# A gated linear attention and an ELU layer on one core: weights' range tested from a second reading, logarithm sums ahead of the arctangent, state products in another order

## The chip, the cores and the metric

The kernel runs on one core of a Trainium2 chip. The metric is the device time of one execution in microseconds (us). Two kernels are compared, the one before the change and the one after it. The engines are TensorE (PE; its weight loads are listed as PEld), VectorE (DVE), ScalarE (ACT), GpSimd (POOL) and the queue of SyncE (SP), which issues most DMAs. All five run their own instructions in order and wait for each other by semaphores.

## The reference

For 4 batches, 8 heads, 768 positions and 48 channels a complex gate with modulus at most 0.999 carries a 48 x 48 state, and the layer behind it is an ELU between two matrices whose entries are 64-bit floats:

```python
mag = np.sqrt(a_re * a_re + a_im * a_im)
scale = np.minimum(mag, 0.999) / (mag + 1e-06)
a_re_n, a_im_n = (a_re * scale, a_im * scale)
for t in range(S):
    new_re = ar * S_re - ai * S_im
    new_im = ar * S_im + ai * S_re
    S_re, S_im = (new_re + k_t v_t^T, new_im)
    y[:, :, t] = q_t^T S_re
x = y.transpose(0, 2, 1, 3).reshape(3072, 384)
h = x @ w_in                                  # 384 x 2048, float64
g = np.where(h > 0.0, h, np.exp(np.minimum(h, 0.0)) - 1.0)
out = (g @ w_out).astype(np.float32)          # 2048 x 384, float64
```

## The kernel before, in words

The work is cut into 12 units: a unit u is two batches (n = 0, 1) by 128 positions with all eight heads. The state runs through the units of the same batches in chunks of 64 positions. For each unit the kernel

- loads a (`load_a`), q and k (`load_qk`) and v (`load_v`), each as [128, 2 x 8 x 48] float32;
- turns the gate into a logarithm of its modulus and an angle: `squares` (two squares on ScalarE, their sum on VectorE or GpSimd), `logarithms` (two logarithms and two exponentials on ScalarE, then two products, L622 and L623, on VectorE for units 0 and 1 and on GpSimd for the others), `slopes` (L629 and L632 on VectorE), `noted` (two reductions on VectorE that keep the least real part and the largest imaginary part), `angles` (arctangent on ScalarE), `carried` (L660 on VectorE, adds the angle carried over from the unit before);
- sums angles along the positions (`turns`: matmuls L671 with a triangular matrix, then L676 and L679 on VectorE) and logarithms (`decays`: matmuls L693, four exponentials L698 on ScalarE), takes sine and cosine (`waves`), and multiplies q and k by them (`gated`: L724, L726, q on VectorE, k on GpSimd);
- then, for n = 0 and 1: `transposed` of q and k (PE L746, copied by ScalarE L747; called Tq and Tk in the prediction), `scores` (L754, masked by L759 on VectorE), `states` (L775; L786 on VectorE adds the old state, L787 on GpSimd multiplies it by the decay), `values` (L797 and L804, copied by ScalarE), and `seam` (six small DMAs from GpSimd's queue that put the output into the layout of the next matmul);
- the layer: eight `hidden` steps (L838: 12 matmul records into a PSUM tile `mlp` with three buffers; ELU by L843 and L844 on ScalarE and L845 on VectorE), and eight `project` steps (L854, 8 matmul records).

The matrices are read as pairs of 32-bit words. `fetch` loads one of 14 parts (six of w_in with 1024 columns, eight of w_out with 768 columns) into a staging tile, and `rounded` makes it float32: five instructions on VectorE (L570, L574, L579, L583, L586). With them goes a range test, so that entries below about 2**-15 in the high word's reading, taken as a float32, become zero: ScalarE squares the high words in place (L578), GpSimd compares (L587) and multiplies the result by it (L590). `rounded` is a generator, and `converts(n)` runs it for n steps; `fetches(n)` starts the next n loads.

The order of all instructions is written out by hand. `put(at, fn, ...)` notes a call at a slot, the calls are sorted by slot (ties in the order of noting), and each engine gets its instructions in that order. A unit from 2 on takes 16 slots, in each of which one `hidden` or `project` step of an earlier unit stands. Units 0 and 1 have negative slots, since nothing of the layer can run beside them; the first `hidden` step is in slot 4, the first `project` in slot 20, and Tq of unit 2 in slot 22. In the plan before, unit u's `squares`, `logarithms`, `slopes`, `noted`, `angles`, `carried`, `turns`, `waves`, `decays` and `gated` stand at r + 11, 12, 14, 14, 15, 15, 16, 17, 18 and 19 with r = 16 (u - 2), and its transposes and products from r + 22 on. A `verdict` at the end takes the noted least and largest values; if they are out of range, a general version of the whole kernel (`_general`) runs behind a branch. With these inputs it does not.

Staging tiles, the `g` tiles of the ELU output and the small tiles of the gate (`n`, six buffers) share tags and therefore buffers; `ar`, `ai`, `q` and `k` have one buffer each.

Of the kernel before, what the change touches and what calls it, by code (L numbers as in the profile page):

```python
# [20 lines left out]
LEAST_RE = 0.7  # L21
# [2 lines left out]

TOP, LOW = 0xC0000000, 0x07FFFFFF
F32_EXP = 0xFF800000

LEAST_SQ = 2.0**-30  # L30
WC = 1024
WF = 2


LEVELS = [1, 2, 4, 8, 16, 32, 64]
# [399 lines left out]


@with_exitstack
def kernel(
    ctx: ExitStack,
    tc: tile.TileContext,  # L440
# [47 lines left out]
    least = cst.tile([C, NU], FP32, name="least")  # L488
    most = cst.tile([C, NU], FP32, name="most")
    ln_eps = value(float(np.log(2 * EPS)), "ln_eps")  # L490
    quarter = value(float(np.pi / 2), "quarter")

    def work(shape):
        return ps.tile(shape, FP32, tag="w", bufs=3, name="w")
# [28 lines left out]
        load(u, "v", v, 2, pad=True)  # L523

    G = HP - D
    places = [(j, i, j * HP, (2 * i + j) * D, D) for i in range(NI) for j in range(2)]
    places += [(j, i, j * HP + D, (2 * NI + j) * D + i * G, G) for i in range(NI) for j in range(2)]  # L530
    raw = {}

    def weights_of(kind, m):

        if kind == "in":
            i, f = m % NI, m // NI * WC
            dst = w_in[:, i, f : f + WC]
            t = sb.tile([C, WC, 2], U32, tag="g" + str(m // 2 % 2), bufs=2, name="w64")
            words = t.rearrange("p n two -> p (n two)")
            pairs = [  # L540
                (words[ds(at, n)], moe_w_in[ds(row, n), 2 * f : 2 * (f + WC)])
                for j, i1, at, row, n in places if i1 == i
            ]
        else:
            dst = w_out[:, ts(m, WF)].rearrange("p f n -> p (f n)")
            tag = "w64" if m % 4 < 2 else "g1"
# [12 lines left out]

    def rounded(kind, m):  # L560

        w, dst = raw.pop((kind, m))
        n = dst.shape[-1]
        lo, hi = w[:, :, 0], w[:, :, 1]
        f = sb.tile([C, n], U32, tag="wt", bufs=2, name="wf")
        p = sb.tile([C, n], U32, tag="wt", bufs=2, name="wp")
        yield nc.vector.tensor_scalar(  # L570
            out=f, in0=hi, scalar1=LOW, scalar2=3, op0=ALU.bitwise_and,
            op1=ALU.logical_shift_left,
        )
        yield nc.vector.scalar_tensor_tensor(  # L574
            out=f, in0=hi, scalar=TOP, in1=f, op0=ALU.bitwise_and, op1=ALU.bitwise_or
        )
        size = hi.bitcast(FP32)
        nc.scalar.activation(out=size, in_=size, func=AF.Square)  # L578
        yield nc.vector.tensor_scalar(  # L579
            out=p, in0=f, scalar1=F32_EXP, scalar2=None, op0=ALU.bitwise_and  # L580
        )
        f, p = f.bitcast(FP32), p.bitcast(FP32)
        yield nc.vector.scalar_tensor_tensor(  # L583
            out=p, in0=lo, scalar=2.0**-52, in1=p, op0=ALU.mult, op1=ALU.mult
        )
        yield nc.vector.tensor_tensor(out=dst, in0=p, in1=f, op=ALU.add)  # L586
        yield nc.gpsimd.tensor_scalar(  # L587
            out=size, in0=size, scalar1=LEAST_SQ, scalar2=None, op0=ALU.is_ge
        )
        nc.gpsimd.tensor_tensor(out=dst, in0=dst, in1=size, op=ALU.mult)  # L590


    def flat(t):
# [2 lines left out]
    def products(u):  # L596

        return nc.vector if u < 2 else nc.gpsimd

    def new(tag, bufs=1, shape=None):  # L600
        return sb.tile(shape or [C, NB, H, D], FP32, tag=tag, bufs=bufs, name=tag)

    def squares(u):
        x = nat[u]
        ar, ai = x["ar"], x["ai"]
        x["m2"], sq = new("n", 6), new("n", 6)
        nc.scalar.activation(out=x["m2"], in_=ar, func=AF.Square)
        nc.scalar.activation(out=sq, in_=ai, func=AF.Square)  # L608
        products(u).tensor_tensor(out=x["m2"], in0=x["m2"], in1=sq, op=ALU.add)  # L609

    def logarithms(u):


        x = nat[u]
        ar, ai = x["ar"], x["ai"]
        lm, lr = x["m2"], new("n", 6)
        nc.scalar.activation(out=lm, in_=lm, func=AF.Ln)
        nc.scalar.activation(out=lr, in_=ar, func=AF.Ln)
        e, x0 = new("n", 6), new("n", 6)
        nc.scalar.activation(out=x0, in_=lr, func=AF.Exp, scale=-1.0)  # L620
        nc.scalar.activation(out=e, in_=lm, func=AF.Exp, scale=-0.5, bias=ln_eps)
        products(u).tensor_tensor(out=lr, in0=ar, in1=x0, op=ALU.mult)  # L622
        products(u).tensor_tensor(out=x0, in0=ai, in1=x0, op=ALU.mult)  # L623
        x["e"], x["w"], x["t"] = e, lr, x0

    def slopes(u):
        x = nat[u]
# [236 lines left out]

    def verdict():

        fit, ones = cst.tile([C, NU], FP32, name="fit"), value(1.0, "ones")
        nc.vector.tensor_scalar(
            out=fit, in0=least, scalar1=LEAST_RE, scalar2=None, op0=ALU.is_ge
        )  # L870
        nc.vector.scalar_tensor_tensor(
            out=fit, in0=most, scalar=LEAST_RE, in1=fit, op0=ALU.is_le, op1=ALU.mult
        )
        t = work([1, NU])
# [3 lines left out]
        nc.vector.tensor_scalar(  # L878
            out=needs, in0=n, scalar1=C * NU - 0.5, scalar2=None, op0=ALU.is_lt
        )  # L880


# [42 lines left out]
    def put(at, fn, *args):  # L925
        plan.append((at, len(plan), lambda: fn(*args)))

    def decays_of(u, *at):
        for x, fn in zip(at, (squares, logarithms, slopes, noted, angles, carried)):
            put(x, fn, u)  # L930

    def gates_of(u, *at):
        for x, fn in zip(at, (turns, waves, decays, gated)):
            put(x, fn, u)

    def values_of(u, base):
        for n, at in enumerate([[0, 1, 2, 3, 5], [3, 4, 6, 7, 8]]):
            for x, (fn, *args) in zip(at, (
                (transposed, u, "q", n), (transposed, u, "k", n), (scores, u, n),
                (states, u, n), (values, u, n),  # L940
            )):
                put(base + x, fn, *args)
        put(base + 9, seam, u)
# [30 lines left out]
    for at, n in FETCHES:  # L974
        put(at, fetches, n)
    for at, n in CONVERTS:
        put(at, converts, n)
# [4 lines left out]
    with tc.If(nc.values_load(needs[0:1, 0:1]) > 0):  # L982
        _general(tc, q, k, v, a_re, a_im, w_in, w_out, out)


# [30 lines left out]
```

## Time and profile before

| | |
|---|---|
| median of 3 runs | 831.32 us (829.62 to 831.35) |
| profiled execution | 831.39 us, its span 829.6 us |
| mean granted TensorE clock | 0.952 |
| busy: PE, DVE, ACT, POOL | 720.4, 336.2, 403.0, 307.4 us |
| read from HBM, written | 36.55 MB, 4.79 MB |

The span is from the first to the last instruction. A busy time is the time in which an engine executes; for PE it is partly modelled. A row of a group has its line, engine and operation, the tiles (output <- inputs), shapes and count; then busy time and mean ns of one, then idle time of the engine just before and what ended it. A row of the order in time has start and duration in us and, in brackets, the idle time before it and what released it.

### The profile page before, as it was taken

How to read it: one execution, taken by the hardware profiler on the slowest of the kernel's cores; microseconds unless marked ns; L12 is line 12 of the kernel's file. 1: busy time of each engine (PE TensorE's matmuls, PEld its weight loads, DVE VectorE, ACT ScalarE, POOL GpSimd, SP SyncE). 2: the span in 40 equal slices, each digit the busy share in tenths (PEclk: the TensorE clock that was granted, in tenths of full speed). 3: DMA queues.
4: the chain of work that ended last, by engine and by line, in shares of the span. 5: the costliest groups of instructions: out<-in, count | busy, mean ns of one | idle time of the engine just before them, and what ended most of it. 6: DMA issues, size and time to landing. Idle time of an engine off the chain costs nothing.

```text
span 829.6 us, 12975 instructions
## 1 busy us (share of the span) xinstructions
PE 720.4 (87%) x5406; PEld 532.3 (64%) x5406; DVE 336.2 (41%) x378; ACT 403.0 (49%) x604; POOL 307.4 (37%) x233
## 2 busy tenths in 40 slices
PE   1586438678999999999999999999999999999996
PEld 0465326555658758668668578577577587587773
DVE  4779998743143152242242342332432332331020
ACT  6663214752554554555555655555455556442130
POOL 0436796703343342441540540541541441340100
PEclk9866678889999999999999999999999999999999
DMA  9969425032042042051061150240330430000000
GB/s 166 162 97 210 89 71 124 1 57 49 11 72 49 1 82 39 2 101 21 4 106 13 24 97 2 46 75 2 66 56 1 72 49 2 15 11 1 25 1 24
DMA packets 136076, 43.49 MB, mean 52 GB/s; under 512 B 128536, under 2 KB 133192, under 8 KB 135240
## 3 DMA queue, kind: packets, MB, share of 16 engines
q1 hardware_dynamic: 132160, 41.14, 27.6%
q0 software_dynamic: 3776, 1.36, 1.4%
q8 instruction: 44, 0.72, 0.4%
q14 instruction: 24, 0.20, 0.1%
q10 hardware_dynamic: 72, 0.07, 0.0%
HBM read 36.55 MB, written 4.79 MB: 50 GB/s over the span
## 4 chain that ended last, share of the span: by engine, by line
PE 49%; issue 18%; DVE 12%; ACT 8%; POOL 7%; DMA 3%; SPq 2%; POOLq 0%; ACTq 0%; DVEq 0%
PE mlp L838 21%; PE mlp L854 17%; PE w L746 3%; POOL S L787 3%; PE w L671 2%; DVE wf L574 2%; POOL n L623 2%; POOL n L622 2%; DMA w<-in_moe_w_out_dram 2%; PE w L754 2%; DMA w<-in_moe_w_in_dram 2%; SPq L509 1%; PE w L693 1%; ACT L654 1%; DVE wp L583 1%
## 5 line engine op out<-in xcount | busy, mean ns | idle before, releaser
L838 PE MATMUL mlp<-x,w_in 128*128 128x256 f32 x1152 | 268.0, 388 | 24.3 <-DVE g L845 24.3
L854 PE MATMUL mlp<-w_out,g 128*128 128x384 f32 x768 | 262.9, 492 | 0.0
L838 PEld LDWEIGHTS mlp<-x,w_in 128*128 128x128 f32 x1152 | 219.8, 195 | 59.6 <-DVE g L845 26.5
L854 PEld LDWEIGHTS mlp<-w_out,g 128*128 128x128 f32 x768 | 142.2, 190 | 92.0
L845 DVE SCALAR_TENSOR_TENSOR g<-ee,mlp 128x512 f32<-128x512 f32 x96 | 65.8, 686 | 228.5 <-ACT ee L844 224.5
L843 ACT ACTIVATE ee<-mlp 128x512 f32<-128x512 f32 x96 | 57.1, 595 | 138.3 <-PE mlp L838 136.9
L787 POOL TENSOR_TENSOR S<-S,T 96x384 f32<-96x384 f32 x40 | 48.2, 1206 | 191.2 <-DVE S L786 191.2
L844 ACT ACTIVATE ee<-ee 128x512 f32<-128x512 f32 x96 | 60.5, 630 | 3.0
L786 DVE TENSOR_TENSOR S<-w,S 96x384 f32<-96x384 f32 x40 | 22.1, 552 | 77.0 <-PE w L775 39.2
L671 PE MATMUL w<-n,sum_turns 128*128 128x384 f32 x48 | 22.4, 598 | 32.5 <-ACT n L654 16.8
L746 PE MATMUL w<-ident,qg 128*96 128x128 f32 x192 | 30.2, 297 | 21.6 <-DVE qg L726 15.0
L609 POOL TENSOR_TENSOR n<-n 128x768 f32<-128x768 f32 x10 | 18.1, 1809 | 79.9 <-ACT n L608 79.9
L726 POOL TENSOR_TENSOR kg<-k,cs 128x1536 f32<-128x1536 f32 x10 | 47.1, 4713 | 0.8
L724 POOL TENSOR_TENSOR k<-k,n 128x768 f32<-128x768 f32 x10 | 21.5, 2149 | 68.0 <-ACT n L698 68.0
L775 PEld LDWEIGHTS w<-vn,kg 64*96 64x96 f32 x704 | 37.1, 171 | 12.0 <-issue 9.0
L860 ACT COPY o<-mlp 128x384 f32<-128x384 f32 x24 | 11.5, 478 | 68.5 <-PE mlp L854 68.5
L747 ACT COPY qt<-w 96x512 f32<-96x512 f32 x48 | 26.4, 577 | 35.9 <-PE w L746 35.7
L812 ACT COPY x<-y 128x384 f32<-128x384 f32 x24 | 11.5, 478 | 65.1 <-PE y L804 64.9
L587 POOL TENSOR_SCALAR w<-w 128x768 f32<-128x768 f32 (+1 forms) x14 | 40.3, 2881 | 6.7 <-ACT w L578 5.7
L775 PE MATMUL w<-vn,kg 64*96 64x48 f32 x704 | 40.3, 257 | 2.5 <-ACT n L698 1.7
L578 ACT ACTIVATE w<-w 128x768 f32<-128x768 f32 (+1 forms) x14 | 14.3, 1019 | 51.9 <-DVE wf L574 38.5
L746 PEld LDWEIGHTS w<-ident,qg 128*96 128x96 f32 x192 | 21.9, 135 | 27.3 <-DVE qg L726 16.0
(76 smaller groups left out, 864.3 us busy)
## 6 DMA issues: line engine op xcount, KB each, us to landing
w<-in_moe_w_out_dram SPq DMA_DIRECT2D x8, 768.0 KB
ar<-in_a_re_dram SPq DMA_DIRECT2D x24, 192.0 KB
ai<-in_a_im_dram SPq DMA_DIRECT2D x24, 192.0 KB
w<-in_moe_w_in_dram SPq DMA_DIRECT2D x12, 384.0 KB
q<-in_q_dram SPq DMA_DIRECT2D x24, 192.0 KB
k<-in_k_dram SPq DMA_DIRECT2D x24, 192.0 KB
vn<-in_v_dram SPq DMA_DIRECT2D x24, 192.0 KB
out_dram<-o SPq DMA_DIRECT2D x24, 192.0 KB
```

Source lines behind the costliest of these rows:

```text
L587: yield nc.gpsimd.tensor_scalar(out=size, in0=size, scalar1=LEAST_SQ, scalar2=None, op0=ALU.is_ge)
L671: nc.tensor.matmul(t, lhsT=sum_turns, rhs=x["th"][:, n].rearrange("p h d -> p (h d)"), start=True, stop=True,)
L726: eng.tensor_tensor(out=o, in0=g.rearrange("p n h d -> p (n h) d").unsqueeze(2).to_broadcast(shape), in1=x["cs"], op=ALU.mult,)
L746: nc.tensor.transpose(t[:, h], x[key + "g"][:, n, h0 + h], ident)
L747: nc.scalar.copy(out=o[:, h0 : h0 + 4], in_=t)
L775: nc.tensor.matmul(g[:, h], lhsT=x["kg"][ts(c, L), n, h], rhs=vn[u % 2][ts(c, L), n, h, 0:D], start=True, stop=True,)
L787: nc.gpsimd.tensor_tensor(out=new_s, in0=new_s, in1=wide, op=ALU.mult)
L838: nc.tensor.matmul(t[:, e], lhsT=w_in[:, i, ts(f + e, C)], rhs=x["x"][:, i], start=(i == 0), stop=(i == NI - 1),)
L843: nc.scalar.activation(out=e, in_=t, func=AF.Relu, scale=-1.0)
L844: nc.scalar.activation(out=e, in_=e, func=AF.Exp, scale=-1.0)
L845: nc.vector.scalar_tensor_tensor(out=x["g", f // 8][:, f % 8 : f % 8 + 2], in0=e, scalar=-1.0, in1=t, op0=ALU.add, op1=ALU.max)
L854: nc.tensor.matmul(x["o"], lhsT=x["g", f // 8][:, f % 8, ts(n, C)], rhs=w_out[:, f], start=(f == 0), stop=(f == NF - 1),)
```

## The change

- The range test leaves `rounded`: L578, L587 and L590 are gone, and dst is written by VectorE's addition alone. A part whose small entries would have needed it is now found by a test: from unit 4's slots on (slot 40, then every eighth) `test_fetch` loads a sixteenth of the two matrices again into a staging tile, and seven slots later `test` takes the least absolute value of the high words per partition, one reduction on VectorE. `verdict` compares these 16 columns too, and where one is out of range, a branch first makes the weights anew with the test (`_any_weights`), and then runs `_general`.
- `logarithms` is split: its two products become `ratios`, a slot and a half later. Of its activations the logarithm of the real part comes first. The sum of squares of unit 1 goes from VectorE to GpSimd.
- `decays` comes ahead of `angles`, and `turns` a slot later. In a unit from 2 on: `squares` r + 11, `logarithms` 12, `ratios` 13.5, `slopes` 14.5, `noted` 14.6, `decays` 15, `angles` and `carried` 15.5, `turns` 17, `waves` 17.5, `gated` 19.
- The second half's transposes (n = 1) stand at r + 26 and r + 27 where they stood at r + 25 and r + 26; the rest of the transposes and products stays.
- Units 0 and 1, the weights' loads and the conversions get new slots, from -45 on.

```diff
-        size = hi.bitcast(FP32)
-        nc.scalar.activation(out=size, in_=size, func=AF.Square)
...
         yield nc.vector.tensor_tensor(out=dst, in0=p, in1=f, op=ALU.add)
-        yield nc.gpsimd.tensor_scalar(
-            out=size, in0=size, scalar1=LEAST_SQ, scalar2=None, op0=ALU.is_ge
-        )
-        nc.gpsimd.tensor_tensor(out=dst, in0=dst, in1=size, op=ALU.mult)
+    def test_fetch(m):
+        t = sb.tile([C, WF * DM, 2], U32, tag="w64", bufs=2, name="w64")
+        if m < NR // 2:
+            n = WF * DM // NI
+            nc.sync.dma_start(
+                out=t.rearrange("p (i n) two -> p i (n two)", i=NI),
+                in_=moe_w_in[:, ds(2 * m * n, 2 * n)].rearrange("(i p) n -> p i n", p=C),
+            )
+        else:
...
+    def test():
+        m, t = tested.pop(0)
+        nc.vector.tensor_reduce(
+            out=smallest[:, m : m + 1], in_=t[:, :, 1].bitcast(FP32),
+            axis=mybir.AxisListType.X, op=ALU.min, apply_absolute_value=True,
+        )
...
-        products(u).tensor_tensor(out=x["m2"], in0=x["m2"], in1=sq, op=ALU.add)
+        eng = nc.vector if u == 0 else nc.gpsimd
+        eng.tensor_tensor(out=x["m2"], in0=x["m2"], in1=sq, op=ALU.add)
...
+        nc.scalar.activation(out=x["w"], in_=x["ar"], func=AF.Ln)
         nc.scalar.activation(out=lm, in_=lm, func=AF.Ln)
...
+    def ratios(u):
+        x = nat[u]
+        w, t = x["w"], x["t"]
+        products(u).tensor_tensor(out=w, in0=x["ar"], in1=t, op=ALU.mult)
+        products(u).tensor_tensor(out=t, in0=x["ai"], in1=t, op=ALU.mult)
...
-    FETCHES = [(-32, 1), (-29, 1), (-27, 1), (-26, 1), (-18, 1), (-12, 1), (-10, 2), (-1.5, 1), (0.5, 1)]
-    FETCHES += [(3.5, 1), (5.5, 1), (7.5, 1), (9.5, 1)]
-    CONVERTS = [(-28, 2), (-26, 2), (-25, 2), (-24, 1)] + [(-20 + i, 1) for i in range(12)]
-    CONVERTS += [(-8 + i, 3) for i in range(22)]
...
-        (-31, load_qk, 0), (-30, load_v, 0), (-28, load_a, 1), (-21, load_qk, 1), (-20, load_v, 1),
+        (-44, load_qk, 0), (-44, load_v, 0), (-42, load_a, 1), (-32.8, load_qk, 1), (-23.5, load_v, 1),
-    decays_of(0, -30, -29, -28, -27, -28, -28)
-    gates_of(0, -26, -25, -25, -23)
-    put(-24, warm, 30)
-    values_of(0, -20)
-    decays_of(1, -22, -21, -18.5, -8, -18, -18)
-    gates_of(1, -17, -16, -15.5, -12.5)
-    values_of(1, -10)
+    for at, n in (
+        (-45, 1), (-43, 2), (-41, 1), (-30, 1), (-26, 1), (-24, 2), (-2, 1), (-1, 1),
+        (3.5, 1), (5.5, 1), (10.5, 1), (12.5, 1),
+    ):
+        put(at, fetches, n)
+    decays_of(0, -40, -39, -39, -38, -37.9, -38, -38, -35)
+    gates_of(0, -36.5, -36, -33)
+    put(-34, warm, 30)
+    values_of(0, -32, -31, -30, -29, -26, -28, -27, -25, -24, -23, -22)
+    decays_of(1, -33.5, -32.5, -31.5, -30.8, -8, -30.7, -30.6, -26.5)
+    gates_of(1, -27.5, -27, -22.5)
+    values_of(1, -20, -19, -18, -17, -14, -16, -15, -13, -12, -11, -10)
+    for at, n in (
+        (-37, 3), (-34.5, 2), (-31.6, 3), (-29.5, 2), (-27.2, 3), (-25.5, 3), (-24.5, 2),
+        (-22.2, 2), (-20, 3), (-17, 3), (-15, 3), (-12, 3),
+    ):
+        put(at, converts, n)
+    for i in range(21):
+        put(i - 2, converts, 2)
...
-        decays_of(u, r + 11, r + 12, r + 14, r + 14, r + 15, r + 15)
-        gates_of(u, r + 16, r + 17, r + 18, r + 19)
-        values_of(u, r + 22)
+        decays_of(u, r + 11, r + 12, r + 13.5, r + 14.5, r + 14.6, r + 15.5, r + 15.5, r + 15)
+        gates_of(u, r + 17, r + 17.5, r + 19)
+        values_of(u, *(r + 22 + x for x in (0, 1, 2, 3, 5, 4, 5, 6, 7, 8, 9)))
...
+    for m in range(NR):
+        put(40 + 8 * m, test_fetch, m)
+        put(47 + 8 * m, test)
```

The arguments of `decays_of` are now the slots of `squares`, `logarithms`, `ratios`, `slopes`, `noted`, `angles`, `carried` and `decays`; those of `gates_of` are `turns`, `waves` and `gated`; `values_of` takes the slots of the first half, of the second half (each: q, k, scores, states, values), and of `seam`.

More of the change, by code (lines that the diff above doesn't have):

```diff
@@ L437, with _any_weights @@
 @with_exitstack
+def _any_weights(ctx: ExitStack, tc: tile.TileContext, w_in, w_out, moe_w_in, moe_w_out):
+    nc = tc.nc
+    NI, DF = w_in.shape[1:]
+    NF, DM = w_out.shape[1:]
+    sb = ctx.enter_context(tc.tile_pool(name="sb3", bufs=1))
+    parts = []
+    for i in range(NI):
+        for f in range(0, DF, WC):
+            parts.append((w_in[:, i, f : f + WC], [
+                (at, n, moe_w_in[ds(row, n), 2 * f : 2 * (f + WC)])
+                for i1, at, row, n in _places(NI, HP * 3 // 4) if i1 == i
+            ]))
+    for f in range(NF):
+        parts.append((w_out[:, f], [(0, C, moe_w_out[ts(f, C)])]))
+    for dst, loads in parts:
+        n = dst.shape[-1]
+        w = sb.tile([C, n, 2], U32, tag="w64", bufs=3, name="w64")
+        words = w.rearrange("p n two -> p (n two)")
+        for at, rows, src in loads:
+            nc.sync.dma_start(out=words[ds(at, rows)], in_=src)
+        f = sb.tile([C, n], U32, tag="wf", bufs=2, name="wf")
+        p = sb.tile([C, n], U32, tag="wp", bufs=2, name="wp")
+        for _ in _rounded(nc, w, f, p):
+            pass
+        f, p, hi = f.bitcast(FP32), p.bitcast(FP32), w[:, :, 1]
+        nc.vector.tensor_tensor(out=p, in0=p, in1=f, op=ALU.add)
+        nc.vector.tensor_scalar(
+            out=hi, in0=hi, scalar1=EXP, scalar2=None, op0=ALU.bitwise_and
+        )
+        nc.vector.scalar_tensor_tensor(
+            out=dst, in0=hi, scalar=float(LEAST), in1=p, op0=ALU.is_ge, op1=ALU.mult
+        )
+@with_exitstack
 def kernel(
@@ L541, in weights_of @@
                 (words[ds(at, n)], moe_w_in[ds(row, n), 2 * f : 2 * (f + WC)])
-                for j, i1, at, row, n in places if i1 == i
+                for i1, at, row, n in places if i1 == i
             ]
@@ L878, in verdict @@
         nc.vector.tensor_scalar(
-            out=needs, in0=n, scalar1=C * NU - 0.5, scalar2=None, op0=ALU.is_lt
+            out=needs, in0=n, scalar1=C * (NU + NR) - 0.5, scalar2=None, op0=ALU.is_lt
         )
@@ L928, in decays_of, with values_of @@
     def decays_of(u, *at):
-        for x, fn in zip(at, (squares, logarithms, slopes, noted, angles, carried)):
+        fns = squares, logarithms, ratios, slopes, noted, angles, carried, decays
+        for x, fn in zip(at, fns):
             put(x, fn, u)
     def gates_of(u, *at):
-        for x, fn in zip(at, (turns, waves, decays, gated)):
+        for x, fn in zip(at, (turns, waves, gated)):
             put(x, fn, u)
[L936 to L943, printed above, removed]
+    def values_of(u, *at):
+        fns = (transposed, "q"), (transposed, "k"), (scores,), (states,), (values,)
+        for n in range(NB):
+            for x, (fn, *key) in zip(at[5 * n :], fns):
+                put(x, fn, u, *key, n)
+        put(at[-1], seam, u)
     def layer_of(u, at_h, at_p):
@@ L982 @@
     with tc.If(nc.values_load(needs[0:1, 0:1]) > 0):
+        _any_weights(tc, w_in, w_out, moe_w_in, moe_w_out)
         _general(tc, q, k, v, a_re, a_im, w_in, w_out, out)
```

88 lines of the change are left out of this document (49 added, 39 removed).

## The prediction

> **What bounds the kernel now.** I read the totals and the slices first, then the busy time of three stretches, then the order of TensorE's work at the seams between them.
>
> ```profile
> span 829.6 us, 12975 instructions
> DVE  4779998743143152242242342332432332331020
> ```
> ```profile
> 0.00:124.42 124.42, 60.55 (x624) 49.32 (x624) 98.92 (x89) 55.82 (x74) 66.14 (x48) 0.76 0.75 133
> 124.42:195.62 71.20, 52.47 (x188) 39.34 (x188) 51.36 (x52) 38.92 (x55) 38.23 (x19) 0.87 0.28 53
> 195.62:829.60 633.98, 607.38 (x4594) 443.64 (x4594) 185.91 (x239) 308.26 (x475) 202.99 (x167) 1.00 0.21 37
> ```
> ```profile
> 101.17 9.88 PE L838 MATMUL mlp<-x,w_in 128*128 128x256 f32 x36
> 125.14 4.66 PE L838 MATMUL mlp<-x,w_in 128*128 128x256 f32 x12 [14.09 <-DVE g L845]
> 195.62 1.08 PE L746 MATMUL w<-ident,qg 128*96 128x128 f32 x8 [2.97 <-DVE qg L726]
> 449.41 2.76 PE L838 MATMUL mlp<-x,w_in 128*128 128x256 f32 x12
> ```
>
> The columns of the stretches are length, then busy time of PE, weight loads, VectorE, ScalarE, GpSimd, the granted clock, DMA share and GB/s. There are two kernels in one. From 195.62 us on TensorE is busy 607.4 of 634.0 us at a clock of 1.00: only its gaps can be won. Before that it is not the bound. At 101.17 it has run three hidden steps, all its mlp buffers allow, and then waits 14.09 us for VectorE's first L845. VectorE is busy 98.9 of the first 124.4 us (the slices show 9 and 8 without a break just before), and what fills it is the weight conversion:
>
> ```profile
> L583 DVE SCALAR_TENSOR_TENSOR wp<-w,wp 128x1024 f32<-128x1024 uint32 (+1 forms) x9 | 15.8, 1759 | 0.2
> L574 DVE SCALAR_TENSOR_TENSOR wf<-w,wf 128x1024 uint32<-128x1024 uint32 (+1 forms) x9 | 15.4, 1711 | 0.2
> L570 DVE TENSOR_SCALAR wf<-w 128x1024 uint32<-128x1024 uint32 (+1 forms) x10 | 12.9, 1287 | 1.6 <-DMA w<-in_moe_w_in_dram 1.4
> L586 DVE TENSOR_TENSOR w_in<-wp,wf 128x1024 f32<-128x1024 f32 x6 | 9.7, 1613 | 0.1
> L579 DVE TENSOR_SCALAR wp<-wf 128x1024 uint32<-128x1024 uint32 (+1 forms) x9 | 8.1, 900 | 0.2
> L586 DVE TENSOR_TENSOR w_out<-wp,wf 128x768 f32<-128x768 f32 x3 | 3.4, 1137 | 0.1
> ```
>
> That is VectorE up to 124.42: 46 conversion instructions, 65.3 us, the other work 33.6 us, idle 25.5 us. Their mean times are not what they cost alone:
>
> ```profile
> 16.61 0.68 DVE L570 TENSOR_SCALAR wf<-w 128x1024 uint32<-128x1024 uint32 x1
> 17.33 1.23 DVE L574 SCALAR_TENSOR_TENSOR wf<-w,wf 128x1024 uint32<-128x1024 uint32 x1
> 53.77 1.22 DVE L586 TENSOR_TENSOR w_in<-wp,wf 128x1024 f32<-128x1024 f32 x1
> 130.76 0.56 DVE L570 TENSOR_SCALAR wf<-w 128x768 uint32<-128x768 uint32 x1
> 131.84 2.00 DVE L574 SCALAR_TENSOR_TENSOR wf<-w,wf 128x768 uint32<-128x768 uint32 x1
> 134.46 0.96 DVE L583 SCALAR_TENSOR_TENSOR wp<-w,wp 128x768 f32<-128x768 uint32 x1
> ```
> ```profile
> 130.88 2.14 POOL L590 TENSOR_TENSOR w_out<-w_out,w 128x768 f32<-128x768 f32 x1 [0.16 <-DVE w_out L586]
> ```
>
> L574 takes 1.23 us on 1024 columns with GpSimd idle, but 2.00 us on only 768 while L590 of the range test runs on GpSimd from 130.88 to 133.02; L583, the same kind of instruction on 768, takes 0.96 alone. So GpSimd's part of the conversion is paid on VectorE.
>
> **The change, part by part.**
>
> *Range test out of the conversion.* Gone are ScalarE's L578 and GpSimd's L587 and L590; the five VectorE instructions stay.
>
> ```profile
> L587 POOL TENSOR_SCALAR w<-w 128x768 f32<-128x768 f32 (+1 forms) x14 | 40.3, 2881 | 6.7 <-ACT w L578 5.7
> ```
>  Undisturbed, a w_in part is 0.68 + 1.23 + 0.68 + 1.23 + 1.22 = 5.04 us and a w_out part 0.56 + 0.96 + 0.56 + 0.96 + 0.96 = 4.00 us. The new plan puts 44 steps ahead of the first L845 (32 up to slot -12, two each in slots -2 to 3): six w_in parts, two w_out parts and four steps, 30.2 + 8.0 + 3.0 = 41.3 us where 46 took 65.3. With the other 33.6 us, VectorE has 75 us of work there.
>
> *The start put in another order.* The loads now go w_in part 0, q, k, v, w_in parts 1 and 2, and only then unit 1's a. One part of 1.05 MB has been put ahead of a, 7.9 us at the 133 GB/s of the first stretch, so unit 1's squares on ScalarE start near 38 in place of 29.91:
>
> ```profile
> 29.91 0.84 ACT L607 ACTIVATE n<-ar 128x768 f32<-128x768 f32 x1 [1.74 <-DMA ar<-in_a_re_dram]
> ```
>
> Behind them in ScalarE's queue stand unit 1's logarithms and then the copies of unit 0's transposes; VectorE's ratios of unit 1 wait for the former. One group of three steps stands ahead there, 2.6 us, so I let 5.5 us of the 7.9 reach VectorE. Putting unit 1's sum of squares on GpSimd adds under 1 us to that chain and takes as much off VectorE: nothing. First L845: 75 + 25.5 + 5.5 = 106, against 124.4. Bounds: without any of the old idle time but the first 8 us it would be 88; with the conversions as slow as now 127.
>
> *From the first L845 to Tq of unit 2* (now 71.2 us). Per slot VectorE then has one L845 and two conversion steps, 0.65 + 2 x 0.83 = 2.3 us, less than a hidden step on TensorE (2.76 us in the last row of its order, 2.6 from one start to the next), so TensorE is no longer held by conversions. What it still must do: 13 hidden steps, unit 2's turns and decays, three projections: 13 x 2.6 + 3.0 + 8.1 = 45 us (turns 1.5 and a projection 5.4 / 2, by rows quoted below). It won't reach that, because ScalarE takes over in slots 11 to 19:
>
> ```profile
> L844 ACT ACTIVATE ee<-ee 128x512 f32<-128x512 f32 x9 | 5.7, 630 | 0.2
> L843 ACT ACTIVATE ee<-mlp 128x512 f32<-128x512 f32 x9 | 5.3, 584 | 8.6 <-PE mlp L838 7.2 <-DVE g L845 1.1 <-ACT n L698 0.3
> L844 ACT ACT_TABLE_LOAD x2 | 2.6, 1283 | 0.0
> ```
>
> Eight hidden steps at 1.21 are 9.7 us; unit 2 adds ten activations of 0.84, the four exponentials of decays at half that width (1.6 or so) and six table loads of 1.28 (logarithm, exponential, arctangent, exponential again, sine, exponential again, as many as now), 17.7 us. It starts when hidden step 4 of unit 0's second half is done, at 106 + 5 x 2.6 + 1.2 = 120, and ends at 147; then the last L845, q's two products on VectorE (about 4) and Tq: 152. The chain squares, GpSimd's sum, logarithms, ratios, slopes, arctangent, turns, sine has its own waits in between; I add 5 us for them: 157 against 195.6. Of the 38.6 us I take 37, for loads that may hold VectorE briefly (first rival). Bounds from the rows: TensorE alone gives 151 (a gain of 45); what VectorE saves in the first stretch alone, 65.3 - 41.3, less the later a, gives 18.
>
> The Trainium skill, "ScalarE: Activation LUTs", What ACT_TABLE_LOAD costs, counts about 2.66 us for a switch, 1.28 for the load and a drain of 1.38. By it six switches would end this stretch 8 us later, and the time would be 792. The trace has 1283 ns for the load and 0.0 us of idle time in the row of the loads; I stay with the row, and give the other its place among the rivals.
>
> *Steady units.* Behind 200 us TensorE's own waits are three, all met once a unit:
>
> ```profile
> PE w L671 <- DVE n L660: 10.8, 9, 1.2
> PE y L804 <- POOL S L787: 6.1, 9, 0.8
> PE w L746 <- DVE S L786: 3.3, 7, 0.5
> ```
> ```profile
> 446.79 1.10 PE L775 MATMUL w<-vn,kg 64*96 64x48 f32 x22
> 463.85 1.56 PE L775 MATMUL w<-vn,kg 64*96 64x48 f32 x32
> 470.75 5.43 PE L854 MATMUL mlp<-w_out,g 128*128 128x384 f32 x16
> 477.39 1.53 PE L671 MATMUL w<-n,sum_turns 128*128 128x384 f32 x4 [1.21 <-DVE n L660]
> ```
> ```profile
> 448.33 0.55 DVE L786 TENSOR_TENSOR S<-w,S 96x384 f32<-96x384 f32 x1
> 471.15 0.95 DVE L632 SCALAR_TENSOR_TENSOR n<-n 128x768 f32<-128x768 f32 x1
> ```
> ```profile
> 450.45 0.82 POOL L787 TENSOR_TENSOR S<-S,T 96x384 f32<-96x384 f32 x1 [0.67 <-DVE S L786]
> 465.29 1.81 POOL L622 TENSOR_TENSOR n<-ar,n 128x768 f32<-128x768 f32 x1 [3.84 <-ACT n L620]
> 467.18 1.81 POOL L623 TENSOR_TENSOR n<-ai,n 128x768 f32<-128x768 f32 x1
> ```
>
> All three go. L746 <- L786: Tq of the second half moves one slot behind its states, so a hidden step or projection covers it. L804 <- L787: the ratios (L622, L623) stood on GpSimd at 465.29 to 468.99 just where the state products wanted it; they now come behind. L671 <- L660: turns moves one slot later, 2.6 us, against a wait of 1.21. But decays, now two slots after the states, becomes the next to be late. From the start of states (446.79) to the end of the second state product (451.27) are 4.5 us; the ratios then take 3.7, the two slopes 1.8: 10.0 us until decays may start. TensorE gets there in 463.85 to 470.75 less the 1.0 us that the L804 wait and its refill cost, 5.9, plus one projection of 2.7: 8.6. So 1.4 us of new wait a unit. Old waits 0.5 + 0.8 + 1.2 and about 0.4 of refill after them, less 1.4 and 0.2: 1.3 a unit. With fewer events of the first kind and nothing to win for the last units, whose states are shorter, I count 8 units: 10 us. Bounds: 0, if the new wait is a little over 2.5 us; 20.2, the whole of the three rows, if there is none.
>
> *The second reading.* Sixteen loads of 0.79 MB, one every eight slots from slot 40, and 16 reductions on VectorE, priced by
>
> ```profile
> L641 DVE TENSOR_REDUCE least<-ar 128x1 f32<-128x768 f32 x12 | 11.3, 941 | 0.0
> ```
>
> 15 us on an engine that is busy 186 of the 634 us: nothing, since L845 leaves 1.9 of the 2.6 us of a hidden step free; without that cover, 15. The loads bring 12.6 MB to a queue that moves 37 GB/s there. SP issues each behind a unit's other loads; the test follows seven slots, some 26 us, later, so it waits for nothing. GpSimd's queue is not passed by any of it. The verdict's additional instruction and the second branch not taken: nothing.
>
> **Sum.** 829.6 - 37 - 10 = 782.6 of span; the profiled execution took 831.39, 1.8 more than its span, and stands at the median of 831.32: 784.4.
>
> **The rivals.**
> - *The start gives half of it back.* VectorE is freed, but loads, the late a of unit 1 and ScalarE's queue hold it: first L845 at 115, Tq of unit 2 at 176, gain 20, and with 10 for the units 801. For it: v of unit 1 is now the last load that the start needs, behind 12 MB; at 133 GB/s it lands at 90 us, and VectorE would want its state sums near 77. Against: that rate is a mean over a stretch with a DMA share of 0.75; at the full share it would be 68. 0.18.
> - *The new wait at decays eats the units.* If the chain of 10.0 us is 1.2 longer, nothing is won per unit: 794. For it: GpSimd's rows vary when VectorE runs beside it. 0.12.
> - *The conversion doesn't get faster*, because it is not GpSimd that slows it: no gain in either stretch but the reordering, some 815. For it only that loads run in the same stretch; against it 0.96 and 2.00 us within three microseconds of each other. 0.03.
> - *Slower:* a test heads VectorE's queue before its load has landed, and L845 and the state sums queue behind it, with TensorE after its three buffers (about 5 us). It would take 48 us over 16 tests, 3 us each beyond that cover: loads landing some 34 us after their slot. At 37 + 25 GB/s nothing shows that. 0.03.
> - *A table load costs ScalarE twice its row.* Six times another 1.28 us in slots 11 to 19: 792. Against it the 0.0 us of idle time after the loads. This is the drain that the Trainium skill's page names. 0.02.
> - *ScalarE doesn't bind*, TensorE runs through from the first L845: 776. 0.09.
>
> **How the numbers follow.** The forecast has 0.53: 784.4, its own range 774 to 796. With the rivals of the units and of ScalarE inside and half of the first one's, the range is 768 to 802. A change within 0.2% is about what can't be told from none. Faster 0.95, within 0.2% 0.02, slower 0.03.
>
> **What would show it.** Right: conversion instructions near 1.2, 0.7 and 0.96 us each; GpSimd's busy time down by the 40 of L587 and what L590 takes; the first L845 near 106 and Tq of unit 2 near 157; a period of some 58.8 us where 60.1 was; PE's waits for L660 and L787 gone, one of 1.4 us before the sums of logarithms in their place. Wrong: VectorE idle for over 10 us between 37 and 75, or waiting on w_out's loads; ScalarE idle in slots 11 to 19; a wait of VectorE for DMA before a test's reduction.

## The result, and the profile after

The changed kernel takes 790.25 us (median of 4, 788.88 to 791.23) against 831.34: a ratio of 0.9507, 95% interval 0.9485 to 0.953. The forecast was 784.4 in a range of 768 to 802. Its profiled execution took 789.48 us with a span of 787.3, so 42.3 us of span are to be found. The same three stretches as before, cut at VectorE's first L845 (now line 918) and at Tq of unit 2, lead to them:

```profile
span 787.3 us, 12936 instructions
DVE  4659997521422531531531531531531531430110
```
```profile
0.00:105.94 105.94, 60.83 (x624) 49.38 (x624) 75.61 (x86) 47.78 (x67) 19.55 (x31) 0.81 0.81 154
105.94:164.37 58.43, 48.72 (x189) 38.18 (x189) 41.98 (x54) 34.03 (x48) 13.14 (x8) 0.88 0.28 68
164.37:787.30 622.93, 603.81 (x4594) 443.38 (x4594) 185.79 (x256) 306.57 (x475) 188.83 (x167) 1.00 0.26 57
```

Columns as in the prediction: length, busy time of PE, weight loads, VectorE, ScalarE, GpSimd, granted clock, DMA share, GB/s. 124.42 became 105.94 (-18.5), 71.20 became 58.43 (-12.8), 633.98 became 622.93 (-11.1). VectorE's first stretch has 75.6 us of work where there were 98.9, GpSimd's 19.6 where there were 66.1. The groups of the conversion over the first 200 us of the changed kernel, 14 parts:

```profile
L42 DVE SCALAR_TENSOR_TENSOR wf<-w,wf 128x768 uint32<-128x768 uint32 (+1 forms) x14 | 15.0, 1071 | 0.3
L49 DVE SCALAR_TENSOR_TENSOR wp<-w,wp 128x768 f32<-128x768 uint32 (+1 forms) x14 | 15.0, 1070 | 0.2
L45 DVE TENSOR_SCALAR wp<-wf 128x768 uint32<-128x768 uint32 (+1 forms) x14 | 9.7, 690 | 0.4
L633 DVE TENSOR_TENSOR w_out<-wp,wf 128x768 f32<-128x768 f32 x8 | 9.2, 1151 | 0.2
L39 DVE TENSOR_SCALAR wf<-w 128x768 uint32<-128x768 uint32 (+1 forms) x14 | 9.1, 651 | 0.3
L633 DVE TENSOR_TENSOR w_in<-wp,wf 128x1024 f32<-128x1024 f32 x6 | 7.8, 1308 | 0.2
```

65.8 us in all, 4.7 a part. In the same view of the kernel before, L42 is L574, and the six rows add up to 93.5 us:

```profile
L574 DVE SCALAR_TENSOR_TENSOR wf<-w,wf 128x768 uint32<-128x768 uint32 (+1 forms) x14 | 25.3, 1810 | 0.2
```

The instruction is the same; the range test that ran beside it is gone. TensorE's order at the seams (the [ ] hold what it waited for):

```profile
92.39 10.31 PE L911 MATMUL mlp<-x,w_in 128*128 128x256 f32 x36
106.67 25.26 PE L911 MATMUL mlp<-x,w_in 128*128 128x256 f32 x108 [3.97 <-DVE g L918]
139.68 2.90 PE L766 MATMUL w<-n,sum_logs 128*128 128x384 f32 x4 [7.74 <-DVE n L705]
142.37 6.55 PE L911 MATMUL mlp<-x,w_in 128*128 128x256 f32 x24
150.05 5.34 PE L911 MATMUL mlp<-x,w_in 128*128 128x256 f32 x24
164.37 1.08 PE L819 MATMUL w<-ident,qg 128*96 128x128 f32 x8 [1.24 <-DVE qg L799]
202.32 1.53 PE L766 MATMUL w<-n,sum_logs 128*128 128x384 f32 x4 [1.44 <-DVE n L705]
261.02 1.53 PE L766 MATMUL w<-n,sum_logs 128*128 128x384 f32 x4 [1.44 <-DVE n L705]
```

The wait for the first L845 has gone from 14.09 to 3.97 us, and nine hidden steps then run without a gap where five gaps stood. New is the wait of 7.74 us at unit 2's sums of logarithms (L766, `decays`). From then on a unit takes 261.02 - 202.32 = 58.70 us. What is left of TensorE's waits behind 200 us is one row in place of three:

```profile
PE w L766 <- DVE n L705: 11.5, 8, 1.4
```

### The profile page after: what moved, and what is told of

Same layout as the page of the kernel before. It is cut to its first block, busy times and chain, and to the rows that moved or that the text cites. A ratio compares the mean times of both kernels' runs of the same rounds, so it can differ in the third digit from the quotient of the medians.

```text
span 787.3 us, 12936 instructions
## 1 busy us (share of the span) xinstructions
PE 713.4 (91%) x5406; PEld 530.9 (67%) x5406; DVE 303.4 (39%) x394; ACT 388.4 (49%) x590; POOL 221.5 (28%) x206
## 4 chain that ended last, share of the span: by engine, by line
PE 75%; DVE 8%; POOL 5%; ACT 4%; issue 4%; DMA 2%; SPq 1%; POOLq 0%; DVEq 0%; ACTq 0%
PE mlp L911 29%; PE mlp L927 26%; PE w L819 6%; PE w L848 5%; PE w L827 3%; PE w L766 2%; POOL n L697 2%; POOL n L696 2%; PE w L744 2%; PE y L877 2%; DVE n L705 1%; DMA w<-in_moe_w_in_dram 1%; PE y L870 1%; POOL S L860 1%; DVE wf L42 1%
## 5 line engine op out<-in xcount | busy, mean ns | idle before, releaser
L918 DVE SCALAR_TENSOR_TENSOR g<-ee,mlp 128x512 f32<-128x512 f32 x96 | 66.0, 687 | 216.4 <-ACT ee L917 176.5
L916 ACT ACTIVATE ee<-mlp 128x512 f32<-128x512 f32 x96 | 57.2, 596 | 147.5 <-PE mlp L911 141.7
L860 POOL TENSOR_TENSOR S<-S,T 96x384 f32<-96x384 f32 x40 | 35.5, 888 | 251.4 <-DVE S L859 251.4
L680 POOL TENSOR_TENSOR n<-n 128x768 f32<-128x768 f32 x11 | 19.9, 1813 | 114.3 <-ACT n L678 114.3
L766 PE MATMUL w<-n,sum_logs 128*128 128x384 f32 x48 | 21.3, 568 | 20.7 <-DVE n L705 19.2
L832 DVE TENSOR_TENSOR a<-w,mask 128x512 f32<-128x512 f32 x24 | 16.5, 688 | 59.2 <-PE w L827 59.2
L820 ACT COPY qt<-w 96x512 f32<-96x512 f32 x48 | 25.5, 575 | 27.8 <-PE w L819 27.7
L899 POOL DMA_DIRECT2D x<-y x72 | 35.7, 503 | 4.5 <-ACT y L889 4.5
L758 POOL DMA_DIRECT2D carry<-n x10 | 5.1, 512 | 111.4 <-DVE n L752 93.0
L819 PE MATMUL w<-ident,qg 128*96 128x128 f32 x192 | 27.2, 286 | 9.7 <-DVE qg L799 9.0
L819 PE MATMUL w<-ident,kg 128*96 128x128 f32 x192 | 26.9, 284 | 9.7 <-ACT qt L820 9.6
```

What stands on the lines that cost most here:

```text
L766: nc.tensor.matmul(t, lhsT=sum_logs, rhs=x["l"][:, n].rearrange("p h d -> p (h d)"), start=True, stop=True,)
L819: nc.tensor.transpose(t[:, h], x[key + "g"][:, n, h0 + h], ident)
L820: nc.scalar.copy(out=o[:, h0 : h0 + 4], in_=t)
L860: nc.gpsimd.tensor_tensor(out=new_s, in0=new_s, in1=wide, op=ALU.mult)
L899: nc.gpsimd.dma_start(out=x["x"][ds(j * HP + D, G), i], in_=x["y"][ds(j * HP + i * G, G)])
L916: nc.scalar.activation(out=e, in_=t, func=AF.Relu, scale=-1.0)
```

## Experiments on the cause

**Theory A**: two causes that add up. GpSimd's range test blocked VectorE's conversions (both stretches of the start), and the reordered units trade three waits for one. **Rival B**: the newly planned start makes the gain. **Rival C**: the second reading costs what is still missing. **Rival D**: the units' gain comes from elsewhere.

### Only the test taken out, everything else as before

```diff
-        nc.scalar.activation(out=size, in_=size, func=AF.Square)
...
-        yield nc.gpsimd.tensor_scalar(out=size, in0=size, scalar1=LEAST_SQ, ...)
-        nc.gpsimd.tensor_tensor(out=dst, in0=dst, in1=size, op=ALU.mult)
+        yield True
```

> The kernel before, without the range test in the conversion (its square on ScalarE and its two operations on GpSimd left out; small weights are then not made zero); VectorE's order and all slots as before. Theory A, GpSimd's test blocks VectorE: conversions fall to 5.0 and 4.0 us a part, the first L845 from 124 to about 107, the stretch behind it to Tq of unit 2 from 71 to about 60, steady units as before: about 802 us. Rival B, the new plan of the start makes the gain: 825 or more.

Measured: 801.48 us, ratio 0.9636 (0.962 to 0.9651). Its three stretches, cut at the same events:

```profile
0.00:106.89 106.89, 60.61 (x624) 48.75 (x624) 77.73 (x88) 47.90 (x67) 18.08 (x30) 0.79 0.92 160
106.89:164.41 57.52, 47.91 (x188) 37.45 (x188) 42.89 (x52) 33.80 (x48) 13.15 (x8) 0.94 0.28 55
164.41:799.80 635.39, 609.08 (x4594) 444.37 (x4594) 185.95 (x239) 308.07 (x475) 203.04 (x167) 0.99 0.21 37
```

Tq of unit 2 comes at 164.41, in the changed kernel at 164.37. Taking out the test alone brings the whole gain of the start; the new plan of the start adds nothing to it that can be seen.

### The test put back into the changed kernel

```diff
-        yield from _rounded(nc, w, f, p)
...
+        for i, ins in enumerate(_rounded(nc, w, f, p)):
+            if i == 1:
+                nc.scalar.activation(out=size, in_=size, func=AF.Square)
...
...
+        nc.gpsimd.tensor_scalar(out=size, in0=size, scalar1=2.0**-30, ..., op0=ALU.is_ge)
+        nc.gpsimd.tensor_tensor(out=dst, in0=dst, in1=size, op=ALU.mult)
```

> The changed kernel with the range test put back into the conversion (square on ScalarE, compare and product on GpSimd), second reading kept, all slots new. Theory A: first L845 some 20 us later than in the changed kernel, the stretch behind it some 10 us longer: about 820 us. Rival B: within 5 us of the changed kernel's 790.

Measured: 823.41 us, ratio 0.9887 (0.9865 to 0.9909).

```profile
0.00:123.30 123.30, 63.96 (x624) 52.12 (x624) 92.91 (x85) 56.21 (x76) 67.26 (x48) 0.74 0.67 129
123.30:197.33 74.03, 50.31 (x188) 38.30 (x189) 48.29 (x54) 37.44 (x53) 39.22 (x20) 0.84 0.25 59
```

With the test back, GpSimd has 67.3 us again and Tq of unit 2 stands at 197.33, before the change at 195.62. So the four kernels agree: with the test 195.6 and 197.3, without it 164.4 and 164.4, whatever the plan. B falls.

The test has a part on ScalarE too, the square L578, and both runs move it together with GpSimd's part. The trace of the kernel before tells the two apart:

```profile
97.67 0.69 DVE L579 TENSOR_SCALAR wp<-wf 128x1024 uint32<-128x1024 uint32 x1
97.72 1.15 ACT L578 ACTIVATE w<-w 128x1024 f32<-128x1024 f32 x1 [9.49 <-issue]
98.40 1.23 DVE L583 SCALAR_TENSOR_TENSOR wp<-w,wp 128x1024 f32<-128x1024 uint32 x1
```
```profile
75.01 2.71 POOL L590 TENSOR_TENSOR w_in<-w_in,w 128x1024 f32<-128x1024 f32 x1
75.40 0.93 DVE L641 TENSOR_REDUCE least<-ar 128x1 f32<-128x768 f32 x1
```

Beside the square, which covers L579 whole and the start of L583, the two take what they take alone (0.68 and 1.23 us in the prediction). Beside GpSimd's L590, L574 took 2.00 us (the prediction's rows), but the reduction L641 its usual 0.93. The Trainium skill, "SBUF — State Buffer", Who interferes with whom, names the mechanism: a VectorE instruction with two inputs in SBUF contends with a GpSimd instruction that reads SBUF, one in a two-port mode does too, and the one that comes second is held up until the first has ended; a reduction never contends. The traces agree: L574 at 131.84 ends 0.82 us behind L590, close to the 0.96 us that it takes alone, and L641 is not lengthened.

### No second reading

```diff
-        put(40 + 8 * m, test_fetch, m)
-        put(47 + 8 * m, test)
+    nc.gpsimd.memset(smallest, 1.0)
```

> The changed kernel without the second reading: no test loads and no test reductions, the verdict's 16 columns filled once by GpSimd (the weights' range is then not tested). Theory A, both are hidden under TensorE: the changed kernel's 790 us within 0.2%. Rival C, the 16 reductions on VectorE or their 12.6 MB cost: up to 15 us less, 775.

Measured: 788.8 us, ratio 0.9477 (0.9463 to 0.949), span 787.0. The two intervals overlap, and the medians are 0.2% apart, so a cost of the second reading can't be told from none. The stretch behind Tq of unit 2, in which all of it stands, is 621.6 us here and 622.9 in the changed kernel: 1.3 us, far from 15. The changed kernel's row of the tests:

```profile
L657 DVE TENSOR_REDUCE seen<-w 128x1 f32<-128x768 f32 x16 | 15.1, 945 | 0.0
```

15.1 us of VectorE, at the price of `noted`'s reductions (941 ns) although every second word is skipped, with no idle time before them, so no load was late. C falls.

### Units 3 to 11 in the old order

```diff
-            decays_of(u, r + 11, r + 12, r + 13.5, r + 14.5, r + 14.6, r + 15.5, r + 15.5, r + 15)
-            gates_of(u, r + 17, r + 17.5, r + 19)
+        if u < 3:
...                                              # the two lines as they were
+        else:
+            decays_of(u, r + 11, r + 12, r + 12, r + 14, r + 14, r + 15, r + 15, r + 18)
+            gates_of(u, r + 16, r + 17, r + 19)
+        second = (3, 4) if u >= 3 else (4, 5)
...
```

> The changed kernel, but units 3 to 11 in the old order: ratios with the logarithms, slopes 14, angles 15, turns 16, waves 17, decays 18, transposes of the second half at 25 and 26. Theory A, the reordering trades three waits a unit for a smaller one: period back from 58.7 to 60.1 us, waits for L660, L787 and L786 back, about 801 us. Rival D, the units' gain comes from elsewhere (GpSimd or the table loads): 790.

Measured: 797.74 us, ratio 0.9583 (0.9567 to 0.9598): 7.5 us over the changed kernel, not 11. The third stretch, TensorE's waits behind 200 us, and two turns one unit apart:

```profile
166.55:796.40 629.85, 607.21 (x4594) 443.57 (x4594) 199.88 (x256) 307.91 (x475) 203.01 (x167) 1.00 0.26 57
```

```profile
PE w L744 <- DVE n L733: 10.8, 9, 1.2
PE w L819 <- DVE S L859: 3.3, 7, 0.5
PE y L877 <- POOL S L860: 0.3, 1, 0.3
```
```profile
326.14 1.53 PE L744 MATMUL w<-n,sum_turns 128*128 128x384 f32 x4 [1.22 <-DVE n L733]
385.55 1.53 PE L744 MATMUL w<-n,sum_turns 128*128 128x384 f32 x4 [1.22 <-DVE n L733]
```

Two of the old waits are back to the letter, the third, for the state product (before: 6.1 us in 9 events), is not, and the period is 59.4, not 60.1. This kernel keeps one thing of the new units: ScalarE takes the logarithm of the real part first, which doesn't need GpSimd's sum. The state product then starts 4.4 us after `states` where it started 5.1 us after (463.85 in the prediction's rows), here from the run and below from the kernel before:

```profile
372.73 1.56 PE L848 MATMUL w<-vn,kg 64*96 64x48 f32 x32
```
```profile
377.10 0.82 POOL L860 TENSOR_TENSOR S<-S,T 96x384 f32<-96x384 f32 x1
```
```profile
468.95 0.82 POOL L787 TENSOR_TENSOR S<-S,T 96x384 f32<-96x384 f32 x1
```

Before the change ScalarE's first logarithm waited 0.61 us for that sum; here it follows its table load at once:

```profile
461.49 0.84 ACT L617 ACTIVATE n<-n 128x768 f32<-128x768 f32 x1 [0.61 <-POOL n L609]
```
```profile
369.64 0.84 ACT L688 ACTIVATE n<-ar 128x768 f32<-128x768 f32 x1
```

The period without the test in the old plan is 60.0 us (387.55 to 447.56), here 59.4: the same 0.6 us. So the order of the two logarithms very likely ends that wait; it was not tried by itself. The slots bring the rest: from this kernel to the changed one the third stretch falls from 629.9 to 622.9 us, 6.9 of the 11.1. D falls.

## Experiments on the missing 7 us and on what is left

The stretch from the first L845 to Tq of unit 2 should have been 51 us and is 58.4. The new wait of 7.74 us stands in it. What leads to it in the changed kernel:

```profile
132.51 1.82 POOL L697 TENSOR_TENSOR n<-ai,n 128x768 f32<-128x768 f32 x1
137.71 0.95 DVE L702 SCALAR_TENSOR_TENSOR n<-n 128x768 f32<-128x768 f32 x1
141.33 0.87 ACT L771 ACTIVATE n<-w 128x384 f32<-128x384 f32 x2 [6.52 <-PE w L766]
```

ScalarE works almost without a pause from 121.61 to 134.80 (hidden steps, and squares, logarithms and exponentials of unit 2), then waits 6.52 us for the sums. GpSimd's ratios end at 134.33, but VectorE comes to the slopes (L702) only 3.4 us later, behind conversion steps and an L918.

### Unit 2 three slots earlier

```diff
+        if u == 2:
+            decays_of(u, 8, 9, 10.5, 11.5, 11.6, 15.5, 15.5, 15)
...                                              # else: as it was
```

> The changed kernel with unit 2's squares, logarithms, ratios, slopes and noted three slots earlier (8, 9, 10.5, 11.5, 11.6), all else as it is. Theory A: the stretch from the first L845 to Tq of unit 2 is 58 us and not 51 because the sums of logarithms of unit 2 wait 7.7 us for slopes that stand behind ScalarE's logarithms, GpSimd's ratios and conversion steps; three slots earlier the wait falls below 1 us, TensorE keeps its clock, and the time falls by some 9 us to 781. Rival: ScalarE's total work binds there, as the prediction had it; the wait only moves to the hidden steps and the time stays above 787.

Measured: 789.45 us, ratio 0.9503 (0.9473 to 0.9532): as the changed kernel. TensorE's order and the stretch:

```profile
123.50 2.86 PE L911 MATMUL mlp<-x,w_in 128*128 128x256 f32 x12 [1.33 <-DVE g L918]
132.52 4.54 PE L911 MATMUL mlp<-x,w_in 128*128 128x256 f32 x12 [3.06 <-DVE g L918]
136.90 1.45 PE L766 MATMUL w<-n,sum_logs 128*128 128x384 f32 x4
160.09 1.68 PE L819 MATMUL w<-ident,qg 128*96 128x128 f32 x8 [2.35 <-DVE qg L799]
```
```profile
102.87:160.09 57.22, 49.49 (x189) 38.49 (x189) 40.85 (x54) 33.56 (x48) 13.63 (x8) 0.91 0.28 68
```

The 7.74 us wait is gone (L766 has none), and the stretch is 1.2 us shorter. TensorE now waits for L918 of hidden steps, and for q at the end. Two rows of VectorE show why:

```profile
122.75 0.69 DVE L918 SCALAR_TENSOR_TENSOR g<-ee,mlp 128x512 f32<-128x512 f32 x1 [4.38 <-ACT ee L917]
131.79 0.67 DVE L918 SCALAR_TENSOR_TENSOR g<-ee,mlp 128x512 f32<-128x512 f32 x1
```

The first waited for ScalarE, which had unit 2's logarithms and exponentials to do. The second stood behind conversion steps and unit 2's two slopes and two reductions, although ScalarE had ended its input at 125.02; it ends TensorE's wait of 3.06 us. My theory of this place falls: the wait was where the lateness showed, not what made it. The time and the moved waits are what the rival forecast, and ScalarE's part of it is the first of the two rows.

### Conversions spread, and all three aids together

```diff
-    for i in range(21):
-        put(i - 2, converts, 2)
+    for i in range(25):
+        put(i - 2, converts, 2 if i < 13 else 1)
```

> The changed kernel with the last twelve conversion steps one a slot in slots 11 to 22 (two a slot up to 16 before). Theory A: part of the 7.7 us wait of unit 2's sums of logarithms is conversion steps that stand ahead of its slopes on VectorE, 3.4 us by the trace; it falls to about 5, the time to 787. Rival: only ScalarE and GpSimd's chain counts; the wait stays and so does the time, 790; or projections now wait for w_out, above 792.

Measured: 788.54 us, ratio 0.9471 (0.9451 to 0.9491). The wait fell to 6.14 us where 5 had been expected, the stretch to 57.8. No gain that can be told from the changed kernel.

The second kernel has the spread, unit 2 earlier, and `ratios` on VectorE (below):

> Ratios on VectorE, unit 2 three slots earlier, and the conversion steps spread as in the run beside. Theory A: VectorE's queue (conversions, slopes, the two reductions) held the hidden steps when unit 2 came earlier alone; with both, the stretch from the first L845 to Tq of unit 2 falls from 58 to about 51, the time from 776.8 to about 769. Rival: ScalarE's total binds, the stretch stays above 56 and the time above 774.

Measured: 776.9 us, ratio 0.9331 (0.9309 to 0.9352), which is that of ratios on VectorE alone. Its stretch:

```profile
106.24:164.02 57.78, 49.51 (x189) 38.48 (x189) 39.24 (x54) 33.57 (x48) 10.03 (x6) 0.91 0.29 69
```

With the run of ratios on VectorE below (58.7) these are five versions of the order, 57.2 to 58.7 us each. The 51 us did not come, and the rival's numbers did (above 56 and 774). VectorE is busy 38 to 43 us of the stretch and ScalarE 34, so neither's total binds over the whole of it. I take it that the chain of unit 2 through all engines does, with hidden steps between; that is argued from the rows, not shown, and which link would have to go stays open.

### Ratios on VectorE

```diff
-        products(u).tensor_tensor(out=w, in0=x["ar"], in1=t, op=ALU.mult)
-        products(u).tensor_tensor(out=t, in0=x["ai"], in1=t, op=ALU.mult)
+        nc.vector.tensor_tensor(out=w, in0=x["ar"], in1=t, op=ALU.mult)
+        nc.vector.tensor_tensor(out=t, in0=x["ai"], in1=t, op=ALU.mult)
```

> The changed kernel with the two products of ratios on VectorE for all units (0.96 us each in place of 1.81 on GpSimd). Theory A: the wait of 1.44 us a unit before the sums of logarithms ends with the chain states, state products, ratios, slopes; 1.7 us shorter it is gone, with its refill some 1.6 us in 8 units, and unit 2 gains 2 to 4: about 775 us. Rival: VectorE then holds up the state sums and masks of the slots around it, and less than half comes: above 783.

Measured: 776.83 us, ratio 0.9341 (0.9324 to 0.9359). No row of TensorE waiting is left behind 200 us, and the third stretch is

```profile
164.76:774.80 610.04, 601.74 (x4594) 444.12 (x4594) 206.71 (x274) 306.59 (x475) 162.72 (x149) 1.00 0.27 59
```

12.9 us under the changed kernel's, with TensorE busy 601.7 of 610.0. Unit 2's stretch didn't gain the 2 to 4 us (58.7).

### Unit 1's a, and its v, earlier

```diff
-        (-45, 1), (-43, 2), (-41, 1), ...            # loads of weights
+        (-45, 1), (-43, 1), (-42, 1), (-41, 1), ...
-        ..., (-42, load_a, 1), ..., (-23.5, load_v, 1),
+        ..., (-42.5, load_a, 1), ..., (-24.5, load_v, 1),   # v only in the second kernel
```

> The changed kernel with the loads of unit 1's a put between the second and the third w_in part. Theory A: VectorE's idle time of 7.3 us before unit 1's ratios shrinks to about 2, the first L845 comes some 5 us earlier, near 101, and the time is 785. Rival: w_in's parts, later by a's 0.8 MB, then hold VectorE up instead, or the loads of q, k and v bind: no change, 790.

Measured: 792.62 us, ratio 0.9525 (0.9505 to 0.9545): no gain. VectorE's wait of 7.3 us before unit 1's ratios is gone, and TensorE met this in its place:

```profile
81.11 2.80 PE L848 MATMUL w<-vn,kg 64*96 64x48 f32 x32 [6.41 <-DMA vn<-in_v_dram]
```

v of unit 1 lands at 81 us, between the 68 and the 90 of the prediction's first rival, and VectorE waits 8.5 us for the product that needs it. With v ahead of the first w_out parts:

> The changed kernel with unit 1's a between the second and third w_in part, as in the run that had only this, and unit 1's v ahead of the first two w_out loads. Theory A: with a earlier alone the 5 us were lost again because unit 1's v came last in SP's queue and state sums waited 8.5 us for it; with v 1.6 MB earlier this wait is under 2 us, the first L845 near 101, the time about 785. Rival: the loads as a whole bind the start, no order helps: 790 or more.

Measured: 786.54 us, ratio 0.9437 (0.9394 to 0.948), 3.7 us under the changed kernel, with intervals that just part. Its first L918 stands at 102.94. But the same start stood at 102.9 to 108.5 us in the profiles of the other versions that share it, with the loads a little earlier or later, so this gain is not firm. (Each profile is of one execution.)

### All of it

> All edits: ratios on VectorE, unit 2 three slots earlier, conversion steps spread, unit 1's a and v earlier. Theory A: 776.8 - 8 - 5 = 764 us. Rivals of the runs beside: 772 or more.

Measured: 771.79 us, ratio 0.9281 (0.9261 to 0.9302), the fastest kernel here, 18.5 us under the changed one, but 8 short of the forecast and at the edge of the rivals' 772.

```profile
0.00:103.25 103.25, 59.21 (x624) 47.97 (x624) 77.25 (x85) 47.87 (x67) 20.73 (x31) 0.84 0.87 157
103.25:158.31 55.06, 46.78 (x188) 36.56 (x189) 39.22 (x54) 33.59 (x48) 10.02 (x6) 0.96 0.31 75
```

13.4 us of the 18.5 are the ratios on VectorE. The other 5 came at the start: Tq of unit 2 at 158.3 where the run with ratios alone had 164.8. Its second stretch has the order of the one at 57.78 us and a clock of 0.91; at 0.96 it takes 55.06. So the edit of a and v brings 5.1 us here (776.9 to 771.79) where it brought 3.7 above; 2.7 of them are that clock.

The same without the spread and without v earlier (unit 2 earlier, ratios on VectorE, a earlier):

> The changed kernel with the three edits together: unit 2 three slots earlier, ratios on VectorE, unit 1's a earlier. If they act at different places they add: 790 - 9 - 13 - 5, less 2 counted twice, about 765 us. If they share a cause, 772 or more.

Measured: 778.26 us, ratio 0.9342 (0.9305 to 0.9379): the ratios' gain and nothing more. VectorE there waited 8.4 us for `states`, which v held up as in the run with a earlier alone.

## Why the prediction held, point by point

- *Conversions.* Forecast: 75 us of VectorE work and 31 us of idle time ahead of the first L845, at 106. Measured: 75.6, 30.3 and 105.94. The prices came from rows of the same instruction with GpSimd idle. That the meeting is so close is partly luck, given the spread of some 5 us in that event. VectorE was idle 12.2 us between 37 and 75, over the 10 that the prediction named as a sign of being wrong; the forecast of the event held all the same, since its sum had that idle time in it. GpSimd's busy time fell from 307.4 to 221.5 us.
- *The late a of unit 1.* Forecast: 5.5 us reach VectorE. Its wait before unit 1's ratios was 3.8 us before the change and is 7.3 now, so 3.5 did; other waits added 1.3, and luck closed the sum. With a earlier the wait is gone. But it was no cost that could be had back by itself: v was next.
- *From the first L845 to Tq.* This is the term that was mis-sized: 51 forecast, 58.4 measured, and it is all of the miss and more. The floor of 45 us for TensorE was priced at full clock; the stretch had 0.88, and TensorE was busy 48.7: half of the miss. Its idle time was 9.7 us, 7.7 and 1.2 of it the two waits above, where I had some 6: the other half. "ScalarE takes over in slots 11 to 19" was right for 13 us and wrong for the rest. ScalarE was busy from 121.6 to 134.8, and then idle for 6.5 us, which was one of the prediction's own signs of being wrong; moving unit 2's first steps three slots ahead moved the waits and left the length.
- *Units.* Forecast: a new wait of 1.4 us, a period of 58.8, 10 us in all. Measured: 1.44, 58.70, 11.1. The meeting at 1.4 has luck in it: the sum starts at 446.79, a row that holds 22 of the 32 matmuls, while `states` began at 446.33, so the chain of the kernel before is half a us longer than I read. In the changed kernel it is 4.55 us from `states` (426.91) to the end of the second state product (431.46), close to the 4.5 of the sum. One reason was wrong, very likely: the wait for the state product ends with the order of the logarithms already.
- *Second reading:* nothing forecast, nothing measured that can be told from none.
- *Table loads.* The rival in which each costs twice its row has nothing for it: in slot 18 of the changed kernel a load runs from 157.86 to 159.14 us and its exponential starts at 159.15.

## What to carry to other kernels

Cost an instruction by its row with the neighbour engine idle, not by its mean: here 27.7 of the 93.5 us that VectorE spent on conversions went when GpSimd no longer ran the test beside it. When a chain between engines is what TensorE waits for, count its links at the speed of the engine that has them: two products of 1.81 us each on GpSimd, met once a unit, cost 13 us of the whole; on VectorE, at 0.96 us each, they left TensorE no wait behind 200 us. And a wait that a trace shows is where lateness meets TensorE; taking it away is worth its length only if nothing else in the same slots is late.

## What the runs showed of the hardware

A wait costs more than its length when TensorE's granted clock falls with it. In the wait of 7.74 us the clock went to 0.50 and stayed there until 144 us. Unit 2's sums took 2.90 us where those after a wait of 1.44 us took 1.53, and the next two hidden steps 6.55 us where two later ones took 5.34: 2.6 us more.

How long a wait must be for this, the runs don't settle. In the run with unit 2 earlier a wait of 3.06 us was followed by 0.50 and a hidden step of 4.54 us; the one after 1.33 us stayed at 2.86. A wait of 2.06 us at the same hidden step was followed by 0.50 and 4.54 us in the run with the three aids, and by 1.00 and 2.86 us in the run with all edits:

```profile
135.72 4.54 PE L911 MATMUL mlp<-x,w_in 128*128 128x256 f32 x12 [2.06 <-DVE g L918]
```
```profile
131.71 2.86 PE L911 MATMUL mlp<-x,w_in 128*128 128x256 f32 x12 [2.06 <-DVE g L918]
```

The Trainium skill, "TensorE: Matmul & The Clock Gate", What's actually happening, gives a window of about 3.4 us without work after which the clock is halved. The wait of 7.74 us agrees with it; those of 3.06 and 2.06 us are shorter and saw the clock halved too, so here the measurement goes beyond the page.
